# The last 256 result columns in two halves: SiLU, product, sum and store, on two store queues

## The chip, the cores and the metric

The kernel runs on one core of a Trainium2 chip. Its engines are TensorE (matrix products, PE in the profile, PEld for its weight loads), VectorE (DVE), ScalarE (ACT), GpSimd (POOL) and SyncE (SP), which here only issues DMAs and waits. SyncE, ScalarE and GpSimd can each issue DMAs. The metric is the device time of one execution in microseconds.

## The reference

An input x of 2048 rows and 640 columns is layer-normed. From the normed rows two things are made: s, the real part of a Fourier transform over the hidden and the sequence dimension, given by matrices, and a SwiGLU feed-forward with 1536 hidden units. The result is x plus the product of s and SiLU of the feed-forward. Cut to what matters:

```
xn = layernorm(x)
a = xn @ dft_hid_re.T;  b = xn @ dft_hid_im.T
s = dft_seq_re @ a - dft_seq_im @ b
h = silu(xn @ w_gate) * (xn @ w_up)
return x + s * silu(h @ w_down)
```

## The kernel before, in words

All is kept transposed: result rows are the 640 hidden indices in five blocks of 128 partitions, result columns the 2048 sequence positions in four chunks of TC = 512. Large products are done by one level of Strassen's scheme, and each fp32 product as three products of a high and a low part (the function mm3).

Four stages follow each other on TensorE: seq (the transform over the sequence, four passes), hid_s (the transform over the hidden dimension; it writes s to the DRAM tensor y_dram), and then twice, for j = 0 and j = 1, gate_up (the hidden layer) and down (the product with w_down and the result). The change lies in the function result inside down, for j = 1 only.

Nothing is issued as it is written. Every operation is recorded with a time relative to TensorE's steps (pl.prod for what feeds TensorE, pl.step for TensorE, pl.post for what comes behind it). A planner (Plan.schedule) gives each a start with lanes for each engine and modelled durations; the list is sorted by start, Plan.place lays out the buffers, and a last loop issues the operations in that order. So each engine works through its own list strictly in order, and since all go through the recording class, every instruction of the profile stands on line 82. What stands on line 1418 of the profile is the closing of the program.

At the end of down(1) the Strassen scheme is called with end = True. Its last product p4 is split so that little work is left behind the last matmul: first 256 columns of the last row block (result "d2", at = 0), then two full row blocks (result 21, e = 0 and 1), then the other 256 columns ("d2", at = 256, the bank of PSUM number 7). For each piece result records: loads of the residual (res, from the transposed input xt) and of s (yb, from y_dram), both on SyncE and 8 us ahead; SiLU from PSUM into the buffer fin by ACT; the product with yb and then the sum with res by DVE, in place; and the store to out, for these pieces by SyncE.

At its end the program closes as follows: SyncE walks a list of waits, each entry for one or two counters, until all DMAs and engines are done; then a barrier of all engines follows twice. Each DMA counts up one of eight hardware counters (SyncE's and ScalarE's, named DMAHW0 to DMAHW7, taken in turn by each new DMA) or of eight software counters (GpSimd's, DMASW0 to DMASW7). The list goes through the hardware counters from 0 to 7.

Of the kernel before, what the change touches and what calls it, by code (L numbers as in the profile page):

```python
# [11 lines left out]
AF = mybir.ActivationFunctionType  # L12
ALU = mybir.AluOpType

P = 128
S, D, F = 2048, 640, 1536
TC = 512
# [261 lines left out]
def tile_fnet_swiglu(  # L279
# [16 lines left out]
    nc = Probe(tc.nc)  # L296
# [5 lines left out]
    pl = Plan()  # L302
# [8 lines left out]
    ps = psum.tile([P, 8, TC], F32, name="ps")  # L311
# [3 lines left out]
    def raw(name, a=0, n=None):  # L315
        o, (arena, size) = where[name], pl.size[name]
        n = size - a if n is None else n
        over = arena == "raw" and o >= RAW_KB * 256 - 8
        return space["raw3" if over else arena][:, o + a - over * (RAW_KB * 256 - 8):][:, :n]

    def hl(name, i, a=0, n=None):

        key = name, "hl"[i]
        o, n = where[key], pl.size[key][1] - a if n is None else n
        over = bisect(HL_AT, o) - 1
        return space[("hl", "hl2", "hl3")[over]][:, o + a - HL_AT[over]:][:, :n]
# [21 lines left out]
    def both(dst, *subs):  # L348
        return [(dst, p, s) for s in (subs or (0,)) for p in "hl"]
# [24 lines left out]
    def pair(b):  # L374
        return ps[:, b[0]:b[0] + len(b), :]
# [4 lines left out]
    def pkeys(b):  # L380
        return [("ps", i) for i in b]
# [6 lines left out]
    def combine(dst, b, other, op, a=0, after=0.0):  # L388
        n = len(b) * TC
        pl.post(lambda: nc.vector.tensor_tensor(wide(raw(dst, a, n)), pair(b), wide(raw(other)), op=op),  # L390
                [*pkeys(b), (other, 0)], [(dst, a)], after)
# [881 lines left out]
    def down(j):  # L1273
        names = {}

        def fetch(p, g):
            n = 768 if p[0] == "p" else 384
            name = names[p, g] = pl.buf(("Td", j, p, g), "hl", 2 * n)
            for i in range(2):
                pl.prod(14 - 4 * g, lambda i=i: nc.sync.dma_start(  # L1280
                    hl(name, i).bitcast(F32), d_dram[p, g][:, i * n:i * n + n]), [("dd", p, g, i)], [(name, "hl"[i], 0)])

        def top(p):
            for g in range(2):
                fetch(p, g)
            return (lambda g, kk, e, i: hl(names[p, g], i, kk * 256 + e * P, P)), (lambda g: both(names[p, g]))

        def dop(h):
            p = f"d{h}"
            if (p, 0) not in names:  # L1290
                for g in range(2):
                    fetch(p, g)
            return (lambda g, kk, e, i: hl(names[p, g], i, kk * P, P)), (lambda g: both(names[p, g]))

        def get(q, g):
            name = ("h", j, q % 10 - 1, q // 10)
            return name, 3 * g * TC, (name, "all", g)

        for half in range(2):
            for c in (1, 2):  # L1300
                name = ("h", j, half, c)
                for g in range(2):
                    pl.alias[name, "all", g] = [(name, (3 * g + i) * TC) for i in range(3)]

        def result(q, b, other, op, at=0, w=TC, e=0):
            half, e0 = (int(q[1]), 4) if isinstance(q, str) else (q // 10, 2 * (q % 10 - 1) + e)
            n = len(b) * w
            c = j + 2 * (half - 1)
            late = 0 if j and q in ("d2", 21) else 4
            yb, name, res = (pl.buf((what, j, q, at, e), "raw", n) for what in ("yb", "fin", "res"))  # L1310
            part = lambda ap: ap.rearrange("p (a b) -> p a b", b=w)
            fold = j == 0
            fold or pl.post(lambda: nc.sync.dma_start(
                part(raw(res)), xt[c, e0:e0 + len(b), :, at:at + w].rearrange("k p t -> p k t")), [], [(res, 0)], -8)
            pl.post(lambda: nc.sync.dma_start(
                part(raw(yb)), y_dram[c, e0:e0 + len(b), :, at:at + w].rearrange("k p t -> p k t")),
                [("yd", c, e0 + i) for i in range(len(b))], [(yb, 0)], -8)
            if other is None:
                pl.post(lambda: nc.scalar.activation(part(raw(name)), pair(b)[:, :, at:at + w], AF.Silu), pkeys(b), [(name, 0)])
            else:  # L1320
                combine(name, b, other, op)
                pl.post(lambda: nc.scalar.activation(raw(name), raw(name), AF.Silu), [(name, 0)], [(name, 0)])
            pl.post(lambda: nc.vector.tensor_tensor(raw(name), raw(name), raw(yb), op=ALU.mult),
                    [(name, 0), (yb, 0)], [(name, 0)], late)
            if fold:
                pl.post(lambda: nc.gpsimd.dma_start(
                    part(raw(name)), xt[c, e0:e0 + len(b), :, at:at + w].rearrange("k p t -> p k t"), accum_op=ALU.add),
                    [], [(name, 0)], late + 1)
            else:
                pl.post(lambda: nc.vector.tensor_tensor(raw(name), raw(name), raw(res), op=ALU.add),  # L1330
                        [(name, 0), (res, 0)], [(name, 0)], late + 1)
            pl.post(lambda: (nc.sync if j and q in ("d2", 21) else nc.gpsimd).dma_start(
                out[e0 * P:(e0 + len(b)) * P, c * TC + at:c * TC + at + w].rearrange("(k p) t -> p k t", p=P),
                part(raw(name))), [(name, 0)], [], late + 3, 8)

        strassen(("down", j), [3, 3], get, top, dop, result, j == 1)


# [83 lines left out]
```

## Time and profile before

| what | value |
|---|---|
| time, median of 3 runs | 969.46 us (969.38 to 969.82) |
| time of the profiled execution | 969.83 us |
| its span, first to last instruction | 967.6 us |
| TensorE matmuls busy | 961.7 us (99%) |
| VectorE busy | 734.6 us (76%) |
| ScalarE busy | 488.6 us (50%) |
| last matmul ends | 963.3 us |

Times in rows are in microseconds from the start of the span; a row of instructions grouped by form gives busy time in us and the mean of one in ns, then the idle time ahead of it and what ended that. A row of the chain or of the timeline gives start, length, and what ran. SPq is SyncE's sequencer, where DMA issues show; a DMA row gives the size and the time from issue to landing. In the windows view the columns are the busy time of each engine with the number of its instructions, the granted clock of TensorE, the share of DMA and its rate.

### The profile page before, as it was taken

What the parts mean: (1) busy time and instruction counts of PE and PEld (TensorE: products, weight loads), DVE (VectorE), ACT (ScalarE), POOL (GpSimd) and SP (SyncE); (2) the same over time, 40 slices, a digit from 0 to 9 for tenths busy, and PEclk for the clock granted to TensorE, in tenths of its full rate; (3) what the DMA queues carried; (4) which work ended last, traced back from release to release, by engine and by line L of the source; (5) the groups of instructions that cost most, each with busy time, mean ns of one, the idle gap of its engine ahead of it and who ended that gap; (6) DMA issues with size and microseconds to landing.
All of it is one profiled execution on the core that took longest, in us unless ns stands there. A gap on an engine that the chain in (4) does not pass through costs nothing.

```text
span 967.6 us, 11521 instructions
## 1 busy us (share of the span) xinstructions
PE 961.7 (99%) x4235; PEld 792.0 (82%) x4235; DVE 734.6 (76%) x932; ACT 488.6 (50%) x676; POOL 121.3 (13%) x184
## 2 busy tenths in 40 slices
PE   9999999999999999999999999999999999999998
PEld 5888888888888888888888888888888888888887
DVE  7889668757774687676987898999978666666775
ACT  5686445454545455544356555563446444444341
POOL 1460211011101110111100211210002000000000
PEclk9999999999999999999999999999999999999999
DMA  9997848494938497778673374439699330105793
GB/s 352 283 249 215 233 147 229 152 271 106 231 109 255 109 236 263 208 196 253 170 213 131 141 265 155 168 136 289 222 292 256 99 133 4 55 1 163 240 346 131
DMA packets 64056, 186.50 MB, mean 193 GB/s; under 512 B 6528, under 2 KB 10368, under 8 KB 64000
## 3 DMA queue, kind: packets, MB, share of 16 engines
q1 hardware_dynamic: 45952, 125.45, 39.0%
q0 software_dynamic: 18048, 60.32, 24.2%
q8 instruction: 33, 0.54, 0.2%
q14 instruction: 23, 0.19, 0.1%
HBM read 151.39 MB, written 34.36 MB: 192 GB/s over the span
## 4 chain that ended last, share of the span: by engine, by line
PE 99%; DMA 0%; DVE 0%; ACT 0%; issue 0%; DVEq 0%; ACTq 0%
PE ps L82 99%; DMA xn<-in_x 0%; DVE raw L82 0%; DVE bst L82 0%; DVE sm L82 0%; ACT raw L82 0%; ACT sm L82 0%; DVE mv L82 0%; DVEq L82 0%; ACTq L82 0%
## 5 line engine op out<-in xcount | busy, mean ns | idle before, releaser
L82 PE MATMUL ps<-hl 128*128 128x512 f32 (+1 forms) x3258 | 780.1, 388 | 0.0
L82 PEld LDWEIGHTS ps<-hl 128*128 128x128 f32 x3258 | 610.1, 188 | 126.6 <-DVE hl L82 0.6
L82 DVE TENSOR_TENSOR hl<-raw,hl 128x1024 fp32r<-128x1024 f32 (+5 forms) x360 | 346.5, 994 | 134.3 <-ACT hl L82 94.4
L82 ACT ACTIVATE hl<-raw 128x1024 fp32r<-128x1024 f32 (+6 forms) x416 | 325.0, 826 | 170.3 <-DVE raw L82 84.8
L82 PE MATMUL ps<-hl,hl 128*128 128x512 f32 (+1 forms) x954 | 259.9, 388 | 0.0
L82 ACT ACTIVATE raw<-ps 128x512 f32<-128x512 f32 (+1 forms) x144 | 97.9, 681 | 231.4 <-PE ps L82 225.2
L82 PEld LDWEIGHTS ps<-hl,hl 128*128 128x128 f32 x954 | 179.0, 188 | 36.9
L82 DVE TENSOR_TENSOR raw<-raw 128x1024 f32<-128x1024 f32 (+7 forms) x216 | 178.6, 849 | 19.8 <-ACT raw L82 15.5
L82 DVE TENSOR_TENSOR raw<-ps,raw 128x512 f32<-128x512 f32 (+1 forms) x95 | 77.2, 814 | 48.4 <-PE ps L82 47.6
L82 DVE TENSOR_TENSOR raw<-raw,raw 128x512 f32<-128x512 f32 (+3 forms) x50 | 44.2, 892 | 6.5 <-ACT raw L82 4.3
L82 ACT ACTIVATE hl<-xn 128x1024 fp32r<-128x1024 f32 (+3 forms) x61 | 42.2, 723 | 13.6 <-PE ps L82 9.1
L82 POOL DMA_DIRECT2D p_dram<-raw x24 | 16.4, 686 | 251.4 <-DVE raw L82 215.7
L82 ACT ACTIVATE raw<-raw 128x512 f32<-128x512 f32 (+1 forms) x30 | 21.5, 718 | 46.7 <-DVE raw L82 46.7
L82 DVE TENSOR_TENSOR hl<-xn,hl 128x1024 fp32r<-128x1024 f32 (+3 forms) x50 | 40.8, 833 | 4.0 <-PE ps L82 3.9
L82 POOL DMA_DIRECT2D raw<-in_cs x36 | 32.5, 984 | 57.7 <-DMA raw<-in_cs 29.1
L82 DVE SCALAR_TENSOR_TENSOR hl<-raw,hl 128x256 fp32r<-128x256 f32 (+4 forms) x56 | 32.7, 586 | 4.0 <-ACT hl L82 4.0
L82 POOL DMA_DIRECT2D out<-raw x10 | 6.9, 689 | 226.6 <-DVE raw L82 197.3
L82 POOL DMA_DIRECT2D d_p<-hl x28 | 15.2, 543 | 71.4 <-ACT hl L82 59.6
L82 ACT ACTIVATE xn<-xn,sm,rowst 128x640 f32<-128x640 f32 (+1 forms) x16 | 14.1, 906 | 5.3 <-DVE sm L82 3.6
L82 DVE BATCH_NORM_STATS2 bst<-xn 128x6 f32<-128x320 f32 x32 | 13.7, 479 | 4.0 <-DMA xn<-in_x 4.0
L82 POOL DMA_DIRECT2D y_dram<-raw x12 | 8.2, 683 | 64.6 <-DVE raw L82 46.2
L82 POOL DMA_DIRECT2D raw<-p_dram x8 | 10.1, 1267 | 44.7 <-DVE raw L82 26.3
(42 smaller groups left out, 84.3 us busy)
## 6 DMA issues: line engine op xcount, KB each, us to landing
raw<-in_cs SPq DMA_DIRECT2D x84, 512.0 KB, 7.0
hl<-d_p SPq DMA_DIRECT2D x56, 384.0 KB, 5.0
raw<-in_cs POOLq DMA_DIRECT2D x36, 512.0 KB, 9.8
raw<-in_wb SPq DMA_DIRECT2D x24, 640.0 KB, 4.7
d_p<-hl POOLq DMA_DIRECT2D x28, 384.0 KB, 4.0
p_dram<-raw POOLq DMA_DIRECT2D x16, 512.0 KB, 4.4
raw<-p_dram SPq DMA_DIRECT2D x8, 768.0 KB, 8.5
xn<-in_x SPq DMA_DIRECT2D x16, 320.0 KB, 9.8
```

The lines of the kernel that those rows point to most:

```text
L82: return real(*args, **kw)
```

## The change

For the piece that is recorded last (j = 1 and at = 256), the SiLU, the product, the sum and the store are each recorded twice, for the columns 0 to 127 and 128 to 255 of the piece. The order of recording is SiLU 0, SiLU 1, product 0, product 1, sum 0, sum 1; the store of half 0 goes to SyncE and the store of half 1 to ScalarE. The loads of res and yb stay whole. In the names, m is 128 and raw(name, a, m) is a slice of the buffer.

```
+            if j and at:
+                m = w // 2
+                for i in range(2):
+                    pl.post(lambda a=i * m: nc.scalar.activation(
+                        raw(name, a, m), ps[:, b[0], at + a:at + a + m], AF.Silu), pkeys(b), [(name, i)])
+                for other, op in ((yb, ALU.mult), (res, ALU.add)):
+                    for i in range(2):
+                        pl.post(lambda a=i * m, other=other, op=op: nc.vector.tensor_tensor(
+                            raw(name, a, m), raw(name, a, m), raw(other, a, m), op=op), [(name, i), (other, 0)], [(name, i)])
+                for i, queue in enumerate((nc.sync, nc.scalar)):
+                    pl.post(lambda a=i * m, queue=queue: queue.dma_start(
+                        out[e0 * P:e0 * P + P, c * TC + at + a:c * TC + at + a + m], raw(name, a, m)), [(name, i)], [], late + 3, 8)
+                return
```

How the engines' lists change, at their ends (the branch is the end of an engine's own work; its line number alone differs). First VectorE, whose last instructions make the last piece; raw is the large buffer in SBUF that holds fin, yb and res, and the brackets name the counters that an instruction waits for:

```order
 L82 TENSOR_TENSOR raw<-raw 128x512 [waits DMAHW0_49,DVE_49]
-L82 TENSOR_TENSOR raw<-raw 128x256 [waits DMAHW3_49,Activation_49]
-L82 TENSOR_TENSOR raw<-raw 128x256 [waits DMAHW4_49,DVE_49]
-L1418 UNCONDITIONAL_BRANCH
+L82 TENSOR_TENSOR raw<-raw 128x128 [waits DMAHW3_49,Activation_49]
+L82 TENSOR_TENSOR raw<-raw 128x128 [waits Activation_49]
+L82 TENSOR_TENSOR raw<-raw 128x128 [waits DMAHW4_49,DVE_49]
+L82 TENSOR_TENSOR raw<-raw 128x128 [waits DVE_49]
```

Two instructions of 256 columns become four of 128, product, product, sum, sum; each sum still waits for its product, but another instruction lies between them.

Then ScalarE, whose last instructions are the last SiLU out of PSUM (ps) and now also a store:

```order
 L82 ACTIVATE raw<-ps 128x512 [waits DMASW2_49,PE_49]
-L82 ACTIVATE raw<-ps 128x256 [waits PE_49]
-L1418 UNCONDITIONAL_BRANCH
+L82 ACTIVATE raw<-ps 128x128 [waits PE_49]
+L82 ACTIVATE raw<-ps 128x128
+L82 DMA out<-raw 128x128 [waits DMAHW0_49,DVE_49]
```

The store of half 1 is the only DMA that ScalarE issues in the program. It stands behind everything else on ScalarE and takes hardware counter 0.

Last SyncE, whose list ends with the stores:

```order
 L82 DMA out<-raw 128x512 [waits DMAHW5_49,DVE_49,Activation_49]
 L82 DMA out<-raw 128x512 [waits DMAHW6_49,DVE_49,Activation_49]
-L82 DMA out<-raw 128x256 [waits DMAHW7_49,DVE_49,Activation_49]
-L1418 UNCONDITIONAL_BRANCH
+L82 DMA out<-raw 128x128 [waits DMAHW7_49,DVE_49]
```

SyncE's last store is half as wide and keeps its place and its counter, 7. TensorE's and GpSimd's lists are the same, and so is everything ahead of these rows.

## The prediction

> **What bounds the kernel now.** I read the share line of the chain of waits on the page first, then the span cut in three by the windows view, and then the last pieces of the chain in order of time.
>
> ```profile
> PE 99%; DMA 0%; DVE 0%; ACT 0%; issue 0%; DVEq 0%; ACTq 0%
> ```
>
> ```profile
> core 0: us, PE busy (x) PEld busy (x) DVE busy (x) ACT busy (x) POOL busy (x), PEclk, DMA share, GB/s
> 0.00:6.46 6.46, 4.88 (x12) 1.49 (x12) 2.05 (x8) 2.39 (x4) 1.00 (x9) 1.00 0.72 219
> 6.46:963.30 956.84, 956.84 (x4224) 790.53 (x4224) 731.66 (x923) 485.81 (x671) 120.34 (x175) 1.00 0.64 193
> 963.30:967.60 4.30, 0.01 (x1) 0.00 (x0) 0.85 (x2) 0.38 (x1) 0.00 (x0) 0.75 0.25 93
> ```
>
> ```profile
> 6.46 956.86 PE ps L82 x4224
> 963.32 0.02 issue
> 963.34 0.39 ACT raw L82
> 963.74 0.02 issue
> 963.76 0.44 DVE raw L82
> 964.20 0.02 issue
> 964.22 0.42 DVE raw L82
> ```
>
> TensorE sets the end without a gap for 956.84 of 967.60 us, at a granted clock of 1.00. Nothing of the change is issued before TensorE's last matmul, so those 956.84 us and the 6.46 ahead of them stay as they are. What can move is the last row of the windows, 4.30 us: SiLU, product, sum, store, and the closing of the program. Within it the chain names one ACT and two DVE instructions up to 964.64 us. What comes behind shows in SyncE's rows: the issue of the last store, its landing, and the closing waits.
>
> ```profile
> 964.71 0.33 SPq L82 DMA_DIRECT2D out<-raw  x1
> ```
>
> ```profile
> out<-raw SPq DMA_DIRECT2D x1, 128.0 KB, 1.9
> ```
>
> ```profile
> L1418 SPq EVENT_SEMAPHORE  x7: 28/28/28, 965.1 to 965.5; - x7
> ```
>
> ```profile
> L1418 SPq EVENT_SEMAPHORE  x3: 17/17/28, 966.6 to 967.5; - x3
> L1418 SPq DRAIN  x3: 7/7/7, 966.7 to 967.0; - x3
> ```
>
> So the tail before is: SiLU 963.34, DVE 963.76 to 964.64, issue 964.71, landing 1.9 later at 966.6, and 1.0 of closing barrier to 967.6. Of the landing, 0.33 is the issue itself. The edit can take at most something out of these 4.30 us, of which 2.9 are landing and barrier.
>
> **The change part by part.** All times below are on the scale of this profiled execution: span 967.6, its own time 969.83, so 2.2 us lie outside the span. That execution is 0.37 above the median of 969.46, so I work out a difference and set it on the median.
>
> *SiLU in halves.* The rows of ACT by form:
>
> ```profile
> L82 ACT ACTIVATE raw<-ps 128x512 f32<-128x512 f32 x113 | 67.4, 598 | 161.0 <-PE ps L82 155.2 <-DVE raw L82 2.3 <-ACT hl L82 1.9
> L82 ACT ACTIVATE raw<-ps 128x256 f32<-128x256 f32 x2 | 0.8, 375 | 1.6 <-PE ps L82 1.6
> L82 ACT ACTIVATE hl<-xn 128x128 fp32r<-128x128 f32 x8 | 2.4, 294 | 0.0
> ```
>
> From 512 to 256 columns the price falls by 223 ns, so a line through the two gives 375 - 112 = 263 ns for 128 columns out of PSUM. The 128x128 row reads SBUF and bounds it from above with 294. ACT's back-to-back starts are closer than its durations:
>
> ```profile
> 925.32 2.85 ACT L82 ACTIVATE hl<-raw 128x1536 fp32r<-128x1536 f32 x2
> ```
>
> ```profile
> L82 ACT ACTIVATE hl<-raw 128x1536 fp32r<-128x1536 f32 x10 | 14.4, 1480 | 3.7 <-DVE raw L82 3.7
> ```
>
> Two of 1480 ns take 2.85 us together, so the second starts 1.37 us after the first, 0.11 before its end. The halves then run 963.34 to 963.60 and 963.49 to 963.76: the first is ready 0.12 earlier than the whole was, the second about 0.03 later.
>
> *Product and sum in halves.* Four DVE instructions take the place of two:
>
> ```profile
> L82 DVE TENSOR_TENSOR raw<-raw 128x256 f32<-128x256 f32 x2 | 0.9, 426 | 0.6 <-ACT raw L82 0.5
> L82 DVE TENSOR_TENSOR raw<-raw 128x512 f32<-128x512 f32 x1 | 0.7, 691 | 0.0
> ...
> L82 DVE TENSOR_TENSOR hl<-xn,hl 128x128 fp32r<-128x128 f32 x8 | 2.2, 273 | 0.0
> ```
>
> ```profile
> 903.96 3.42 DVE L82 TENSOR_TENSOR raw<-raw 128x1536 f32<-128x1536 f32 x2
> ```
>
> ```profile
> L82 DVE TENSOR_TENSOR raw<-raw 128x1536 f32<-128x1536 f32 x3 | 5.2, 1750 | 0.0
> ```
>
> I take 280 ns for one of 128 columns: near the row of just that shape, 273, and with a line through the tail's 691 (512 columns) and 426 (256) as the upper end, 426 - 132 = 294. The pair of 1536 columns, neither of which needs the other, takes 3.42 where two of 1750 ns in series would take 3.50: the second starts 0.08 before the first ends. Before, the sum needs the product that has just left, and starts 0.02 behind its end. After, the interleaving puts an independent instruction between, so starts come every 0.20. Product 0 at 963.64 (the 0.04 behind ACT that the chain shows), product 1 at 963.84, sum 0 at 964.04 (product 0 ended at 963.92), sum 1 at 964.24. Their ends: sum 0 at 964.32, sum 1 at 964.52. Against 964.64 the first half is 0.32 earlier, the second 0.12. The waits for the loads of y and x stand in front of product 0 and sum 0 as before, and those loads were issued before 957.
>
> *The store in two halves on two queues.* SyncE issues at 964.32 + 0.07 = 964.39, as it did 0.07 behind DVE before; ACT at 964.59 against 964.71. Nothing is queued behind either but the closing. ACT issues no DMA before, so its issue price has no row. The nearest are SyncE's 0.33 above, and POOL's:
>
> ```profile
> L82 POOL DMA_DIRECT2D out<-raw x10 | 6.9, 689 | 226.6 <-DVE raw L82 197.3
> ```
>
> I bound ACT's issue by 0.33 and 0.69 and take 0.33, since its transfer is a plain one like SyncE's and POOL's queue is another kind on the page (software). A queue's first transfer may start late. For that SyncE's own first issue, the DMA rate over the first 2 us in 40 slices of 0.05, and two short windows behind the last store:
>
> ```profile
> 0.73 0.38 SPq L82 DMA_DIRECT2D xn<-in_x  x1
> ```
>
> ```profile
> GB/s 0 0 0 0 0 0 0 0 0 0 0 0 0 0 0 0 0 0 0 0 0 0 0 0 0 0 0 0 0 0 0 0 0 0 102 205 102 256 205 102
> ```
>
> ```profile
> 965.20:965.50 0.30, 0.00 (x0) 0.00 (x0) 0.00 (x0) 0.00 (x0) 0.00 (x0) 0.86 0.00 0
> 965.50:965.80 0.30, 0.00 (x0) 0.00 (x0) 0.00 (x0) 0.00 (x0) 0.00 (x0) 0.50 0.79 283
> ```
>
> The queue's first transfer moves data behind 34 empty slices, at 1.70, 1.0 after its issue; the last one at 965.5, 0.8 after its issue. Cold costs 0 to 0.2.
>
> Size helps a little: SyncE's stores of 256 KB land in 2.4, those of 128 KB in 2.0 (the last 1.9), so 64 KB should land in 1.7.
>
> ```profile
> out<-raw SPq DMA_DIRECT2D x2, 256.0 KB, 2.4
> out<-raw SPq DMA_DIRECT2D x2, 128.0 KB, 2.0
> ```
>
> The two stores meet on the DMA engines, 0.2 apart, which gives back 0 to 0.2. I take 0.1 for this and 0 for cold: ACT's half lands at 964.59 + 1.7 + 0.1 = 966.4, 0.2 before the old landing; SyncE's half lands ahead of it, at about 966.1. Bounds: 966.3 with none of these costs; 967.3 with the slow issue (+0.36), no gain by size (+0.2), the full meeting (+0.2) and cold (+0.2).
>
> [...]
>
> *The closing list.* SyncE ends with a list of waits over the DMA counters, hardware counters 0 to 7 in rising order. Before, the last store stood on counter 7, so its wait was the end of the list, and the others had been walked while it was in flight: the row of seven, 965.1 to 965.5, is 0.4 over six steps, 0.07 each. Now SyncE's half has counter 7 and ACT's, the later one, counter 0. Behind the wait for it stand seven more entries, all long fulfilled but each to be walked: 7 x 0.07 = 0.5 us, no longer under a transfer. This is an estimate from those rows; it falls to 0 if ACT's half isn't the last to land.
>
> *Sum:* landing -0.2, list +0.5, closing barrier unchanged at 1.0: span 967.9, and 969.46 + 0.3 = 969.7 us. The ends are -0.3 (landing 966.3, no list) and +1.2 (landing 967.3, list 0.5). Nothing is costed at nothing but TensorE's part, whose cover is that all of this is issued after it.
>
> What a measurement of this kernel can tell from no change is about 0.2%, 1.9 us. Every term above is far below.
>
> **The rivals.**
>
> *The tail shortens.* If the list is walked in time, for example because both halves land together, only the gain of 0.2 to 0.3 is left: 969.2 us. For it speaks that DVE's ends and the size row both point down; against it the 0.07 per entry.
>
> *The halves run in series.* If DVE doesn't start one before the former has ended, four of 0.28 with 0.02 between them end at 963.64 + 1.18 = 964.82, 0.18 behind the old end, and sum 1 is 0.30 later than I said: 970.0 us. Against it stands the 1536-column pair at 3.42, for it that the pair is long, and that in the new code each instruction carries a wait. The Trainium skill states this as a rule: VectorE: DVE Perf Modes, section The DRAIN you can't avoid, has the next instruction held until the pipeline is empty; the pair's 3.42 against 3.50 doesn't agree.
>
> *Slower, by the second queue.* The kernel before has one hardware queue that moves data (SyncE's), the new one two. The time outside the span, 969.83 - 967.6 = 2.2 us, holds the opening and closing of the execution. If that part grows with each queue used, and a second costs as much again, the result is 969.7 + 2.2 = 971.9 us, slower. It decides from 1.7 us on beside my 0.3. For it there is only that no row splits the 2.2; against it, that these 2.2 hold everything outside the span for five engines and two queues already, so a whole 2.2 for one more is the extreme. The Trainium skill (Runtime: NRT & Kernel Launch, section The launch sequence) lets launch overhead depend on engine count and DMA setup; no run so far shows it here.
>
> *Faster by over 0.2%* would need 1.9 us out of a tail in which 1.0 is barrier and 1.9 landing; arithmetic and its gaps are 1.3 in all. No mechanism gives it.
>
> **How the numbers follow.** My forecast (landing a little earlier, list longer) 0.58, the shorter tail 0.22, the series 0.15, the second queue 0.04, 0.01 for what I haven't seen on the fast side. The first three lie within 0.2%: same 0.95, slower 0.04, faster 0.01. Predicted is the likeliest, 969.7. The range takes the three cases, 969.2 to 970.0, with the ends of -0.3 and +1.2 (969.2 to 970.7), and goes 0.3 further down for the spread of runs (the time before went from 969.38 to 969.82), which the upper end, where four costs come together, holds already: 968.9 to 970.7.
>
> **What would show it.** In the profile after: the TensorE piece of the chain still 956.8 to 956.9 us long; two ACT rows of about 263 ns and four DVE rows of about 280 ns, ending near 964.5; a DMA issue on ACT's queue near 964.6 of about 0.33; landings of about 1.7 to 1.8 for 64 KB; and seven entries of SyncE's closing list, 0.07 apart, behind the landing of ACT's half, not ahead of it. The prediction is wrong if the piece of TensorE changes length, if ACT's first transfer takes well over 2.5 us to land, or if time minus span leaves 2.2 by over a microsecond.

## The result, and the profile after

| | before | after |
|---|---|---|
| median | 969.70 us (22 runs, 969.38 to 969.90) | 971.22 us (22 runs, 970.81 to 971.68) |
| ratio | | 1.0016, 95% interval 1.001 to 1.0022 |
| profiled execution | 969.83 us | 971.09 us |
| its span | 967.6 us | 968.9 us |
| time outside the span | 2.2 us | 2.2 us |

The change costs 1.5 us, 0.16%: within the 0.2% called no change, but the two sets of runs do not overlap. The forecast was 969.7 with a range up to 970.7, so the time lies 0.5 above the range.

The last pieces of the chain of waits after show start, length and what ran:

```profile
6.50 956.70 PE ps L82 x4224
963.20 0.02 issue
963.22 0.29 ACT raw L82
...
963.53 0.20 DVE raw L82
...
963.74 0.49 DVE raw L82 x2
964.23 0.20 DVEq L1431
```

TensorE's piece is 0.16 shorter than before (956.70 against 956.86), and the arithmetic behind it ends at 964.43, 0.2 earlier than before; 0.12 of this is that SiLU starts earlier. The windows view from the last matmul to the end of the span (here the columns are as in the prediction):

```profile
963.20:968.90 5.70, 0.00 (x0) 0.00 (x0) 0.90 (x4) 0.45 (x2) 0.00 (x0) 0.74 0.21 72
```

What was 4.30 us is 5.70. The timeline of ScalarE, VectorE and SyncE's queue shows where it starts to go (a row marked x2 joins two entries and the time between them; SyncE's two issues take 0.34 and 0.33):

```profile
963.19 1.40 SPq L82 DMA_DIRECT2D out<-raw  x2
...
963.22 0.45 ACT L82 ACTIVATE raw<-ps 128x128 f32<-128x128 f32 x2 [1.55 <-PE ps L82]
...
963.53 0.90 DVE L82 TENSOR_TENSOR raw<-raw 128x128 f32<-128x128 f32 x4 [0.41 <-ACT raw L82]
...
964.46 1.37 ACTq L82 DMA_DIRECT2D out<-raw  x1
```

ScalarE's store is issued at 964.46, but the issue takes 1.37 us, not 0.33. The DMA view from 963 to 970 gives size and time from issue to landing:

```profile
q14 instruction: 3, 0.02, 1.2%
...
out<-raw SPq DMA_DIRECT2D x1, 256.0 KB, 2.7
out<-raw SPq DMA_DIRECT2D x1, 64.0 KB, 2.0
out<-raw ACTq DMA_DIRECT2D x1, 64.0 KB, 2.7
```

ScalarE's 64 KB land 2.7 us after the start of their issue, at 967.15. SyncE's closing entries behind that landing, in three windows (count, shortest/median/longest in ns, first and last start):

```profile
L1431 SPq EVENT_SEMAPHORE  x5: 28/28/28, 967.2 to 967.5; - x5
L1431 SPq EVENT_SEMAPHORE  x3: 28/28/28, 967.8 to 968.0; - x3
L1431 SPq DRAIN  x1: 7/7/7, 968.1 to 968.1; - x1
```

Eight entries, the wait for counter 0 and the seven behind it, stand behind the landing, with a gap of 0.38 after the fifth. The list ends, with the first DRAIN, 0.9 us after the landing.

Read to hundredths from the records of the single instructions, the tail divides so:

| piece of the tail, us | before | after | difference |
|---|---|---|---|
| first SiLU starts to last store's issue starts | 1.37 | 1.24 | -0.12 |
| that issue | 0.33 | 1.37 | +1.04 |
| end of the issue to last landing | 1.55 | 1.31 | -0.24 |
| last landing to the end of SyncE's list | 0.08 | 0.91 | +0.83 |
| end of the list to end of the span | 0.94 | 0.83 | -0.11 |
| sum | 4.27 | 5.66 | +1.39 |

SiLU itself starts 0.12 earlier in this execution, so the span grew by 1.27; the two executions' times differ by 1.26. Before's lies 0.13 above its median and after's 0.13 below, which makes the 1.52 of the medians. So two things have to be explained, the slow issue and the long list.

In the same window, 963.9 to 964.9, the DMA view after has a row that before does not have. After:

```profile
q1 hardware_dynamic: 135, 0.25, 63.6%
q14 instruction: 1, 0.01, 4.3%
```

and before:

```profile
q1 hardware_dynamic: 142, 0.26, 67.7%
```

The row q14 is a transfer of 8 KB of instructions, at 964.22, just ahead of ScalarE's issue. Before, the corresponding one came at 967.92, behind the end of the span, after ScalarE's DRAIN in the barrier had come late.

### The profile page after: what moved, and what is told of

Same layout as the page of the kernel before. It is cut to its first block, busy times and chain, and to the rows that moved or that the text cites. A ratio compares the mean times of both kernels' runs of the same rounds, so it can differ in the third digit from the quotient of the medians.

```text
span 968.9 us, 11527 instructions
## 1 busy us (share of the span) xinstructions
PE 961.6 (99%) x4235; PEld 792.0 (82%) x4235; DVE 734.7 (76%) x934; ACT 488.5 (50%) x677; POOL 122.4 (13%) x184
## 4 chain that ended last, share of the span: by engine, by line
PE 99%; DMA 0%; DVE 0%; ACT 0%; issue 0%; DVEq 0%; ACTq 0%
PE ps L82 99%; DMA xn<-in_x 0%; DVE raw L82 0%; DVE bst L82 0%; DVE sm L82 0%; ACT sm L82 0%; ACT raw L82 0%; DVE mv L82 0%; DVEq L1431 0%; DVEq L82 0%; ACTq L82 0%
## 5 line engine op out<-in xcount | busy, mean ns | idle before, releaser
L82 ACT ACTIVATE raw<-ps 128x512 f32<-128x512 f32 (+2 forms) x145 | 98.1, 678 | 232.1 <-PE ps L82 226.0
L82 DVE TENSOR_TENSOR raw<-raw 128x1024 f32<-128x1024 f32 (+8 forms) x218 | 178.8, 843 | 19.4 <-ACT raw L82 15.4
L82 POOL DMA_DIRECT2D raw<-in_xt x6 | 6.9, 1296 | 71.6 <-DVE raw L82 71.6
```

The costliest lines, as they stand in the source:

```text
L82: return real(*args, **kw)
```

## The experiments

All times are medians, with the median of the kernel before on the same chip beside them; it was 969.70, 969.71, 969.74 and 969.71 in the four groups. Since these agree within 0.04, medians of different groups are compared, the change's 971.22 too. All differences to before are under 0.2%, and but for the first kernel below every interval of the ratio reaches 1.0. What the text rests on is therefore the traces, and medians of kernels whose executions do not overlap; where they do overlap, it says so.

### First group: ScalarE's queue, a cold queue, or the counters?

The first suspicions were that ScalarE's first DMA issue is slow as such, and that the list is long because the last store stands on counter 0. Four kernels separate them.

**Both half stores by SyncE.**

```
-                for i, queue in enumerate((nc.sync, nc.scalar)):
+                for i, queue in enumerate((nc.sync, nc.sync)):
```

> Both half stores issued by SyncE, one behind the other, in place of one by SyncE and one by ScalarE; all else as in the change. Theory (the 1.5 us come from ScalarE's DMA issue, 1.37 us against SyncE's 0.33, and from the closing list walked behind the landing on counter 0, 0.9 us): the second store is issued at about 964.65 on the change's scale and lands 1.75 later at 966.4 instead of 967.1, the list still follows behind it: 971.2 - 0.7 = 970.5 us, span 968.2. Rival (only ScalarE's issue costs, the list is free): 969.6 us. Rival (small stores as such cost it): stays at 971.2 us.

Measured: 970.97 us, ratio to before 1.0013 (1.0004 to 1.0022), beside 971.22 for the change. SyncE's second issue in the timeline:

```profile
964.47 1.27 SPq L82 DMA_DIRECT2D out<-raw  x1
```

None of the three values came; nearest, 0.23 off, is the rival of small stores, which the kernels with 8 copies below answer. The slow issue is not ScalarE's: SyncE, which had issued over 260 DMAs by then, took 1.27 us for the same step. Here too a row q14 stands at the place, at 964.52.

**The halves in arithmetic, one store.**

```
-                for i, queue in enumerate((nc.sync, nc.scalar)):
-                    pl.post(... queue.dma_start(out[... m columns], raw(name, a, m)) ...)
+                pl.post(lambda: nc.sync.dma_start(
+                    out[e0 * P:e0 * P + P, c * TC + at:c * TC + at + w], raw(name)), [(name, 0), (name, 1)], [], late + 3, 8)
```

> SiLU, product and sum in halves as in the change, but one store of 256 columns by SyncE behind both sums, as before. Theory: VectorE ends 0.1 us earlier behind the last matmul than before, the store keeps counter 7 at the end of the closing list and is issued by SyncE, so 969.7 - 0.1 = 969.6 us. Rival (the halves on ScalarE and VectorE cost part of the 1.5 us): 970.0 us or more.

Measured: 969.84 us, ratio 1.0003 (0.9994 to 1.0012), between the theory's 969.6 and the rival's 970.0; the executions overlap with those of before. The one store takes counter 7 and is issued in 0.33. The transfer of instructions came at 964.85, 0.25 after the start of that issue, which was not held; but one of the 16 DMA engines landed its part 0.4 after the others, at 966.81 against 966.33 to 966.47.

**The counters shifted by one**, so that ScalarE's store stands on counter 7. An earlier store of 128 KB (the piece "d2", at = 0) goes from SyncE to GpSimd; the last loads of y and x, which stand behind it in SyncE's list, go out earlier for it.

```
-            pl.post(lambda: (nc.sync if j and q in ("d2", 21) else nc.gpsimd).dma_start(
+            pl.post(lambda: (nc.sync if j and q == 21 else nc.gpsimd).dma_start(
```

> The change, with the store of the first 256 columns of the last row block (issued some 9 us earlier, at 954.5) moved from SyncE to GpSimd, whose DMAs use the software counters: from there on each hardware counter is one lower, so ScalarE's last store stands on counter 7, the end of the closing list, and SyncE's on 6. ScalarE's issue is as in the change. Theory (the list behind counter 0 costs 0.8 us): 971.2 - 0.8 = 970.4 us, with the row of waits walked before the landing. Rival (list free): 971.2 us.

Measured: 970.52 us, ratio 1.0009 (1.0 to 1.0018).

```profile
964.45 1.50 ACTq L82 DMA_DIRECT2D out<-raw  x1
```

The issue is as slow as in the change, and the list is gone: it ends 0.09 after the landing, not 0.91. Of the 0.82 that this saves in the span 0.44 came back in the barrier, which is 1.27 long instead of 0.83: between two of GpSimd's steps there stand 0.33 us where the change has 0.03, and the step behind takes 0.15 more. In the time this does not show, since 1.77 lie outside the span here, 0.44 less than in the change (more on this below).

**A DMA on ScalarE's queue ahead of the last.** The store of the first full row block (result 21, e = 0; the expectation calls it the fourth) is moved from SyncE to ScalarE, so the last one is no longer ScalarE's first.

```
-            pl.post(lambda: (nc.sync if j and q in ("d2", 21) else nc.gpsimd).dma_start(
+            pl.post(lambda: (nc.scalar if j and q == 21 and not e else nc.sync if j and q in ("d2", 21) else nc.gpsimd).dma_start(
```

> The change, with the store of the fourth row block (issued at 959.2, 4 us ahead of the end) by ScalarE instead of SyncE, so that the last store isn't the first DMA that ScalarE issues. Counters as in the change. Theory A (the first issue on ScalarE is slow, 1.37 us, with 8 KB of instruction data fetched beside it; a second is like SyncE's): first issue 1.3 to 1.4, last issue 0.33, landing 0.9 to 1.0 sooner: 970.2 to 970.3 us. Theory B (each issue on ScalarE takes 1.37 us): stays at 971.2 us.

Measured: 970.20 us, ratio 1.0005 (0.9996 to 1.0014). That is the time which theory A named, but not for its reason. ScalarE's two issues:

```profile
959.10 0.37 ACTq L82 DMA_DIRECT2D out<-raw  x1
...
964.44 0.34 ACTq L82 DMA_DIRECT2D out<-raw  x1
```

The last issue is fast. But so is the first, 0.37, on a queue that had moved nothing. Theory A has the first at 1.3 to 1.4. A cold queue is not the cause; in this kernel, with one store more on ScalarE, the row q14 had moved to 960.63, between the two issues.

### Second group: a transfer of instructions, moved out of the way

In the trace of before, the 8 KB transfers that fit ScalarE stand where about 65, 193, 322, 445, 580, 703, 833 and 961 of its instructions have been recorded: one about every 128. The change gives ScalarE three instructions more (a SiLU, a wait, the store; 961 recorded before, 964 after), and the last transfer, which belonged to the closing before, now falls ahead of it. The theory: this transfer, where it falls on the last stores, holds an issue. Then a few small instructions anywhere earlier on ScalarE must bring the transfer forward and take the 1 us away, on either queue. So the next kernels put N copies of one column into a scratch tile that nothing reads, on ScalarE at the start of the program:

```
+    for i in range(N):
+        nc.scalar.activation(scratch[:, i:i + 1], sm[:, 5, :1], AF.Copy)
```

**The change with 8 copies:**

> The change, with eight tiny ScalarE instructions (copies of 128x1 into a scratch tile that nothing reads) in ScalarE's idle time at the start of the program. Nothing else moves; every later ScalarE instruction stands eight places further down its list. Theory P (place in the list: an 8 KB instruction transfer that ScalarE's list sets off near its 959th instruction falls among the last stores, at 964.2, and holds up ScalarE's issue): the transfer moves ahead of 961, ScalarE's issue falls from 1.37 to 0.35, the landing to about 966.2, 971.2 - 0.95 = 970.2 us. Theory C (a first DMA on ScalarE is slow by itself, at the end of the program): issue stays at 1.37, 971.2 us.

Measured: 970.15 us, ratio 1.0004 (0.9995 to 1.0013); 1.07 less than the change, for eight instructions more. The DMA view from 952.8 to 953.5 now has the row, 963.9 to 964.9 does not:

```profile
q14 instruction: 1, 0.01, 3.4%
```

The timeline of ScalarE's queue, and SyncE's list:

```profile
964.40 0.37 ACTq L82 DMA_DIRECT2D out<-raw  x1
```

```profile
L1433 SPq EVENT_SEMAPHORE  x8: 27/28/28, 966.1 to 966.9; - x8
L1433 SPq DRAIN  x2: 7/7/7, 967.0 to 967.1; - x2
```

The issue is back at 0.37, and what is left of the loss is the list of eight, which ends 0.89 behind the landing. Two small stores are in this kernel as well, so they do not cost the 1 us.

**Both stores by SyncE, with 8 copies:**

> Both half stores by SyncE, with the same eight ScalarE instructions at the start. Without them SyncE's second store took 1.27 us to issue, at 964.47, beside an instruction transfer from 964.52 to 965.61. Theory P: that transfer is ScalarE's and holds up any engine's issue; moved away, SyncE's second issue takes 0.35 and 971.0 falls by 0.8 to 0.9: 970.1 us. Theory Q (a store behind two others of the same queue waits for room, whatever ScalarE does): stays at 971.0 us.

Measured: 970.25 us, ratio 1.0006 (0.9997 to 1.0015); 0.72 less than without the copies.

```profile
964.60 0.38 SPq L82 DMA_DIRECT2D out<-raw  x1
```

SyncE's second issue falls from 1.27 to 0.38 by eight instructions on another engine. Together with the kernel above, and with the store moved to ScalarE in the first group, this shows for both queues that the place in ScalarE's list decides whether the issue is slow.

**The kernel before with 1 copy**, which should bring the transfer into its last store:

> The kernel before with a single one of the tiny ScalarE instructions at the start, nothing of the change. Theory P: ScalarE's instruction transfer, which in the kernel before comes only with the closing barrier (967.9), is set off one instruction earlier, by the closing drain at 963.4, and runs about 964.8 to 965.8, on one DMA engine together with the last store; one engine's part of the store lands 0.4 late: 970.1 us. Any theory in which the number of ScalarE instructions doesn't matter: 969.7 us.

Measured: 969.56 us, ratio 1.0 (0.9991 to 1.0009), where 970.1 was expected.

```profile
964.44 0.33 SPq L82 DMA_DIRECT2D out<-raw  x1
```

The transfer did come, at 964.54, but the issue had begun 0.10 ahead of it and took 0.33, and the store landed on all 16 DMA engines together (966.20 to 966.31). Four of the eleven executions were at 970.0 to 970.26, the others at 969.39 to 969.63, so the loss may come in some executions only; the one profile, of an execution of 969.43, can't show that. The theory's rule was too simple: a transfer beside an issue is not enough.

**One store, with 8 copies:**

> Halves on ScalarE and VectorE, one store by SyncE, with the eight ScalarE instructions at the start. Without them one DMA engine's part of the last store landed 0.4 to 0.5 behind the other fifteen (966.81 against 966.33), beside an instruction transfer from 964.85 to 965.81. Theory P: the sixteen parts land together, 969.84 - 0.4 = 969.4 to 969.5 us, below the kernel before (969.7). Otherwise: 969.8 us.

Measured: 969.48 us, ratio 0.9998 (0.9989 to 1.0007), 0.36 less than without the copies, though the executions of the two overlap (969.39 to 969.94, and 969.42 to 970.48). All 16 parts land together (966.14 to 966.25).

### Third group: the prices, one by one

**The kernel before with 8 copies**, the control for them:

> Control: the kernel before with the eight tiny ScalarE instructions at the start and nothing of the change. In the kernel before ScalarE's transfer falls into the closing barrier, where ScalarE's drain starts at 967.255 behind the others. Theory: 0.1 us less, 969.6 us; the kernels with eight are to be compared with this one. If the eight instructions cost at the start: above 969.7 us.

Measured: 969.63 us, ratio 0.9999 (0.999 to 1.0008). Eight copies without the change move nothing that can be measured, though they take ScalarE's transfer out of the barrier.

**The kernel before, with its last store on counter 0.** The load of yb for the last piece is cut into two DMAs, which turns the counters by one.

```
+            for o, m in ((0, w // 2), (w // 2, w // 2)) if j and at else ((0, 0),):
+              pl.post(lambda o=o, m=m: nc.sync.dma_start(
+                raw(yb, o, m) if m else part(raw(yb)),
+                y_dram[c, e0, :, at + o:at + o + m] if m else ...
```

> The kernel before with one load cut in two: the s values of the last 256 columns come in two DMAs of 128 columns. Both are issued long before they are needed (953 to 956); the effect is that each later DMA takes the next hardware counter, so the last store stands on counter 0 instead of 7. Theory (list walked behind the landing): 0.8 to 0.9 more, 970.5 us. Rival (list free): 969.7 us.

Measured: 970.47 us, ratio 1.0008 (0.9999 to 1.0017); 0.73 above before, where 970.5 was expected.

```profile
L1420 SPq EVENT_SEMAPHORE  x8: 28/28/28, 966.5 to 967.3; - x8
L1420 SPq DRAIN  x2: 7/7/7, 967.3 to 967.4; - x2
```

The landing is at 966.44 and the list ends 0.88 later. Nothing else of the change is in this kernel, so this is the price of the list alone. Seven steps of 0.07 would be 0.5; the rest is one gap of 0.38 between two entries. Before has the same gap, from 965.51 to 965.87, hidden under the store; its last three entries ahead of the landing are here:

```profile
L1418 SPq EVENT_SEMAPHORE  x3: 28/28/28, 965.4 to 965.9; - x3
```

**The change without the store of the second full row block** (result 21, e = 1; the expectation calls it the fourth), whose 256 KB are on the DMA engines when ScalarE issues; these 512 columns of its rows are not written. One theory had the issue wait for this backlog, the other for the instructions alone.

```
+            if j and q == 21 and e:
+                return
```

> The change without the store of the fourth row block of the last chunk (its 512 columns are left out of the output), the 256 KB store that is in flight when the two half stores are issued. ScalarE's list is the same, so its instruction transfer falls at about 964.2 again. Theory B (the issue waits for room: behind the transfer one DMA engine falls back with the 256 KB store's part and can't take a third DMA's entries): with only one store ahead ScalarE's issue takes 0.35 to 0.4. Theory T (the transfer holds up the issue by itself, whatever else is in flight): 1.3 to 1.5. In both the last store stands on counter 7, so the list costs nothing.

Measured: 970.27 us, ratio 1.0006 (0.9996 to 1.0016).

```profile
964.58 1.43 ACTq L82 DMA_DIRECT2D out<-raw  x1
```

With only SyncE's 64 KB ahead of it the issue is as slow as ever, so the backlog falls. These 64 KB landed on all 16 DMA engines within 0.14 (965.83 to 965.97), so a DMA engine that has fallen behind is not needed either. One DMA less also turns the counters, so ScalarE's store is on counter 7 and the list ends 0.10 behind its landing: the two costs come apart once more, the issue's without the list's.

**All costs taken away:** the change, the counters shifted, 8 copies on ScalarE, and 10 small memsets into the scratch tile on GpSimd.

```
-            pl.post(lambda: (nc.sync if j and q in ("d2", 21) else nc.gpsimd).dma_start(
+            pl.post(lambda: (nc.sync if j and q == 21 else nc.gpsimd).dma_start(
+    for i in range(10):
+        nc.gpsimd.memset(scratch[:, 6 + i % 2:7 + i % 2], 0.0)
+    for i in range(8):
+        nc.scalar.activation(scratch[:, i % 6:i % 6 + 1], sm[:, 5, :1], AF.Copy)
```

> The change with both costs taken away: the eight tiny ScalarE instructions at the start (so that ScalarE's instruction transfer falls at about 953) and the store of the first 256 columns of the last row block by GpSimd (so that ScalarE's last store stands on counter 7, the end of the closing list, and SyncE's on 6). Ten tiny GpSimd writes into the same scratch tile at the start keep GpSimd's own list from a transfer in the closing barrier. Theory (1.5 us = about 1.0 from the issue and 0.8 from the list, less 0.2 to 0.3 of gain from the halves): 970.15 - 0.8 = 969.3 to 969.4 us, 0.3 to 0.4 below the kernel before. Rival (the list is not the second cost): 970.1 us.

Measured: 968.92 us (968.67 to 969.09), ratio to before 0.9991 (0.9982 to 1.0), 0.4 to 0.5 less than expected, and 2.3 less than the change as it was made. None of its eleven executions is as slow as the fastest of before (969.45). Timeline and the cores view:

```profile
964.16 0.37 ACTq L82 DMA_DIRECT2D out<-raw  x1
```

```profile
core 0: 966.9 us, clock 0.999
```

The tail is 3.97 from SiLU to the end of the span, against 4.27 before and 4.15 in before with 8 copies. The rest of the gain lies outside the span: 968.67 for the profiled execution less 966.89 is 1.78, where before has 2.22. In the fourteen traces up to here the outside is 2.21 to 2.24 in twelve, and 1.77 and 1.78 in the two that moved a store to GpSimd (this one and the shifted counters). The DMA view behind the span's end, for before 968.2 to 969.2, still has this row:

```profile
q14 instruction: 1, 0.01, 3.1%
```

In this kernel there is none from 966.9 to 968.6.

### Fourth group: the gap in the list, the lone issue, and the time outside the span

Three things were open. First the gap: in the traces it falls behind SyncE's 463rd or 464th recorded instruction, wherever that stands in the list, and in most of them an 8 KB transfer follows 0.63 to 0.68 after it. That looks like SyncE's own step into a new block of instructions. In the same way the 0.44 outside could be GpSimd's step, which falls behind the end of the span. And the held issue had always been the second of two.

**The change with 8 copies, and 8 small DMAs by SyncE** in the middle of the program, where SyncE is idle:

```
+        if t >= 520 and padded < 8:
+            nc.sync.dma_start(scratch[:1, padded:padded + 1], x[:1, padded:padded + 1])
+            padded += 1
```

> The change with 8 copies on ScalarE (970.15 us), and besides 8 DMAs of 4 bytes by SyncE in a quiet place in the middle of the program, which leave all later DMAs on the counters that they had. In thirteen of the fourteen traces so far a gap of 0.34 to 0.38 us stands in SyncE's closing list behind SyncE's 463rd or 464th recorded instruction, wherever in the list that falls, and a transfer of 8 KB of instructions comes some 0.65 after it. Theory S: the gap is SyncE's own step into a new block of instructions. Then the 8 DMAs bring it forward, out of the list; the list behind the landing is seven steps of 0.07 without a gap, 0.5 instead of 0.85, and the time is 969.8. Rival: the gap belongs to one of the waits in the list (to its counter). Then it stays, the list stays 0.85 long, and the time is 970.15.

Measured: 969.86 us, ratio 1.0001 (0.9992 to 1.001), beside 970.15 without the eight DMAs. The whole list behind the landing:

```profile
L1436 SPq EVENT_SEMAPHORE  x8: 28/28/28, 966.1 to 966.5; - x8
L1436 SPq DRAIN  x1: 7/7/7, 966.6 to 966.6; - x1
```

The executions overlap (969.54 to 970.18, and 970.01 to 970.30), but the trace is clear. There are still eight entries behind the landing, and the gap is gone: seven steps of 0.06 and one of 0.07 to the DRAIN, 0.49 in all, the 0.5 of the prediction. So the gap is not a matter of a wait in the list, but of where SyncE's instructions stand.

**The kernel before with 10 small memsets on GpSimd**, no store moved:

```
+    for i in range(10):
+        nc.gpsimd.memset(scratch[:, i % 2:i % 2 + 1], 0.0)
```

> The kernel before, with 10 memsets of one column on GpSimd at the start, and no store moved. Before has a transfer of instructions 0.98 us behind the end of its span and 2.2 us outside the span; the two kernels in which GpSimd got more instructions have 1.77 and 1.78. Theory G: GpSimd steps into a new block of instructions behind the end of the span, which costs 0.44; the memsets bring that forward. Then no transfer lies 0.98 behind the end, 1.78 us lie outside the span, and the time is 969.25. Rival: what counted was the store that moved from SyncE to GpSimd in those two. Then 2.2 lie outside and the time is 969.7.

Measured: 969.33 us, ratio 0.9996 (0.9987 to 1.0006). Its profiled execution took 969.65:

```profile
core 0: 967.9 us, clock 1.000
```

Outside lie 1.77 us (969.65 less 967.88). The medians differ by 0.38, with executions that overlap. A longer list on GpSimd does it, without a moved store.

**The change without SyncE's half of the last store**, so that ScalarE's issue has none beside it:

```
-                for i, queue in enumerate((nc.sync, nc.scalar)):
+                for i, queue in ((1, nc.scalar),):
```

> The change without SyncE's half of the last store (columns 0 to 127 of the piece are left out of the output), so that ScalarE's store is the only one behind the transfer of instructions at 964.2 to 964.5. In the change and its variants the held issue was always the second of two, 0.2 apart. Theory H: any issue that starts about 0.2 behind the start of the transfer is held. Then ScalarE's issue takes 1.3 to 1.5 us; its store is on counter 7, so that the list is not seen, and the time is 970.2 to 970.4. Rival: it takes two issues close together. Then ScalarE's takes 0.34 to 0.37 and the time is 969.2 to 969.4.

Measured: 970.48 us, ratio 1.0008 (0.9998 to 1.0017).

```profile
964.52 1.79 ACTq L82 DMA_DIRECT2D out<-raw  x1
```

Alone, it is held too, so two issues close together are not needed. But 1.79 and 970.48 lie above the 1.3 to 1.5 and the 970.2 to 970.4 of the theory, and the transfer's row stands at 964.77 here, 0.25 after the issue's start, not 0.2 before it: the issue is held, but not in the order that the theory asks for.

**The change as it is, with 8 copies on ScalarE, 10 memsets on GpSimd and 7 small DMAs by SyncE**, seven so that ScalarE's store comes to stand on counter 7:

```
+    for i in range(10):
+        nc.gpsimd.memset(scratch[:, 7:8], 0.0)
+    for i in range(8):
+        nc.scalar.activation(scratch[:, i % 6:i % 6 + 1], sm[:, 5, :1], AF.Copy)
...
+        if t >= 520 and padded < 7:
+            nc.sync.dma_start(scratch[:1, padded:padded + 1], x[:1, padded:padded + 1])
+            padded += 1
```

> The change as it is, with no store moved, and idle instructions on three engines: 8 copies on ScalarE, 10 memsets on GpSimd, and 7 DMAs of 4 bytes by SyncE in the middle of the program, which also turn the counters so that ScalarE's store is on counter 7. Theories S and G together with what was shown before: no held issue, no list behind the landing, 1.78 us outside the span: 968.8 to 969.0, as the kernel with the shifted store had (968.92). If G falls, 2.2 outside and 969.3 to 969.4.

Measured: 968.87 us (968.57 to 969.31), ratio 0.9992 (0.9983 to 1.0001), and 1.77 outside the span. This is the change of the text, untouched, and 25 instructions that do nothing: 2.35 us less than the change alone. All its executions lie below all 31 of before beside it (969.43 to 970.09), 0.84 between the medians, though the interval of the ratio reaches no change.

## Why the prediction was right and wrong

**TensorE's part unchanged:** right in substance. Its piece is 956.70 against 956.86, just below the 956.8 to 956.9 that the prediction named, and it starts 0.04 later; before with 8 copies had 956.46, so this varies by more between executions of the same work.

**SiLU, product and sum in halves:** right, nearly to the hundredth. SiLU took 278 and 271 ns (263 was said), the four DVE instructions 284 to 293 (280), and they started 0.20 apart (963.53, .74, .94, 964.15). The last sum ended 1.21 after the first SiLU's start, against 1.30 before. The rival of halves in series did not appear: starts are 0.20 apart at durations of 0.29. The rule that the prediction took from the Trainium skill, VectorE: DVE Perf Modes, section The DRAIN you can't avoid, is limited there: a next op that is not held starts earlier. These starts agree with that.

**ScalarE's issue, bounded by 0.33 and 0.69, taken at 0.33:** this is the step that failed. It took 1.37, outside both bounds. Without this cost the time lies in the range: the change with 8 copies took 970.15. The price of an issue that is not held was right: 0.34 to 0.38 in the kernels in which the transfer of instructions falls elsewhere (with a DMA ahead of it, with 8 copies, with 8 copies and shifted counters, and with everything padded). Missed was a different cost: the part on the change counted what each engine's list gains, and put three instructions more on ScalarE at the price of their own execution. It did not ask where the next 8 KB of ScalarE's list would be fetched; in the sum this stood at nothing, without a reason. Before had a hint. At 84.55 SyncE's issue in its timeline took four times the usual:

```profile
84.55 1.28 SPq L82 DMA_DIRECT2D raw<-in_cs  x1
```

and its DMA view from 84.4 to 84.7 has TensorE's transfer of 16 KB beside it:

```profile
q8 instruction: 1, 0.02, 19.4%
```

Seven of SyncE's 264 issues there took over 1 us, and three of the seven stand beside such a row; what made the other four slow is not known. The bounds came from the last store and a mean, and left these out.

**Cold queue, 0 to 0.2, taken at 0:** right within 0.05. Where ScalarE's first store came early, 256 KB, it was issued in 0.37 and landed 2.46 after the start of its issue; the same store by SyncE took 2.41 in the change.

**Landing 1.7 for 64 KB and 0.1 for the meeting:** right where the issue isn't held. In the change with 8 copies the two halves land 1.6 and 1.7 after their issues. In the change the landing came 1.31 after the end of the issue, 0.24 less than before.

**The closing list, 7 entries of 0.07, +0.5:** right in mechanism, too small. Alone it cost 0.73 in time (the kernel before on counter 0), and 0.83 in the change's trace. The steps are 0.06 to 0.07, much as said, and 0.5 is what is left where the gap is out of the way (0.49). The row of seven entries that gave the 0.07 ended at 965.5; the eighth entry, 0.36 later, was left out of the price.

**Barrier 1.0 unchanged:** 0.83 against 0.94, as ScalarE's late DRAIN has left it; before with 8 copies has 0.83 too.

**Time outside the span:** 2.2 and 2.2, so the rival of a second queue that costs 2.2 falls.

**The sum.** On the prediction's scale, +0.3 came from -0.2 and +0.5. The tail measured +1.39. The difference of 1.09 is 1.04 from the issue and 0.33 from the list, less 0.16 from the landing and 0.11 from the barrier. Another 0.24 of the miss in time is the base: before was 969.46 in the three runs shown and 969.70 in 22.

**The shorter tail** (969.2) did not come, but its mechanism is there: with the held issue and the list both taken away, the tail is 3.97, 0.18 less than before's with the same copies, where 0.2 to 0.3 was said.

What stays open is how an issue is held, and which. Held were issues that began 0.24 after the row of the transfer (the change; also without the block's store), 0.17 after it (the shifted counters), 0.05 before it (both stores by SyncE) and 0.25 before it (the lone store); not held were those that began 0.03 after (SyncE's in the change), and 0.10, 0.25 and 0.30 before (before with 1 copy; one store; the change with 8 copies and 8 small DMAs). In before, at 728.5, an issue 0.26 after a q14 transfer took 0.43 only. So the row's time does not decide it. What is shown, by moving it on both queues, is that the place in ScalarE's list makes the issue slow; the 8 KB transfer is what the traces show moving with it. That the transfer itself holds the issue is likely but not shown, nor is the way from the one to the other. Before with 1 copy, 0.5 off, stays the miss of this theory.

## What to carry to other kernels

An edit in the last microseconds of a kernel has a price in instruction fetches and in the closing list that no row of its own operations shows. Count the instructions that it adds to each engine, look for the rows of instruction transfers near the end of the trace, and ask which of them move into the last stores; a few idle instructions far ahead move them out again. Here 25 on three engines, seven of which also turn the counters, were worth 2.35 us, where the edit itself shortens the tail by 0.18. And look which counter the last DMA takes: its wait as the first or the last of the closing list was worth 0.7 us.

## What the runs showed of the hardware that was not expected

- ScalarE's instructions came in transfers of 8 KB, about one per 128 recorded instructions, and where one fell among the last stores, an issue took 1.27 to 1.79 us in five kernels, on SyncE's queue or on ScalarE's, instead of 0.33 to 0.38. In two kernels one fell there and no issue was slow. The Trainium skill, Runtime: NRT & Kernel Launch, section Instruction fetch mechanics, has blocks of 16 KiB and calls the cost of a crossing mostly hidden; here the block was 8 KB for this engine, and moving the crossing was worth 1.07 us.
- The place in an engine's list also cost the engine itself: 0.36 to 0.38 us between two of SyncE's closing waits, gone when eight DMAs were added ahead, and 0.4 outside the span that ten memsets on GpSimd removed. That these are steps into a new block of instructions is the likeliest reading. Of the eighteen traces the four with more instructions on GpSimd have 1.77 to 1.78 outside, the other fourteen 2.21 to 2.24.
- In one of the two kernels where such a transfer met a store without holding its issue, one of the 16 DMA engines landed its part 0.4 late, and the median was 0.36 longer than with the transfer moved away (one store, without and with 8 copies; the executions overlap). In the other (before with 1 copy) all 16 landed together.
- A DMA issue by ScalarE took 0.34 to 0.38 us, nearly SyncE's 0.33. The Trainium skill, DMA: Bandwidth & Descriptors, section Issuing engines are not separate DMA queues, says that a second queue saves only the issue, and the traces agree: with 8 copies the two halves landed 1.6 to 1.7 after their issues on one queue as on two.
